# Two transformer layers on one core: three shifts of block 0 summed on TensorE, projections in the order q, q, k, k, v, v, and the first layer norms started elsewhere

## The chip, the core and the metric

The kernel runs on one core of one Trainium2 chip. The metric is the device time of one execution in microseconds; of several executions the median is given. The engines are TensorE (PE, with PEld for its weight loads), VectorE (DVE), ScalarE (ACT), GpSimd (POOL) and SyncE (SP), which here only issues DMAs. ScalarE and GpSimd issue DMAs too, in the same queue as their arithmetic.

## The reference

An activation `x` of 2048 positions x 1024 features (bf16) passes four residual steps: attention, gated MLP, attention, gated MLP, the two of a kind with the same weights. Each step normalizes its input first.

```python
def _A_ref(x, wqkv, wo):                 # H = 32 heads of 32
    W, dil = 8, 2
    qkv = (x @ wqkv) ...                 # q, k, v: heads x positions x 32
    off = jnp.arange(W) * dil
    idx = pos[:, None] - off[None, :]    # position s looks at s, s-2, ... s-14
    logits = einsum("bhsd,bhswd->bhsw", q, k[idx]) * scale
    logits = where(idx >= 0, logits, -1e9)
    o = einsum("bhsw,bhswd->bhsd", softmax(logits), v[idx])
    return o @ wo

def _B_ref(x, W_gate, W_up, W_down):     # 1024 -> 3584 -> 1024
    gate = x @ W_gate; up = x @ W_up
    return (gate * (gate > 0) * up) @ W_down

x = x + _A_ref(_layernorm(x)); x = x + _B_ref(_layernorm(x))
x = x + _A_ref(_layernorm(x)); x = x + _B_ref(_layernorm(x))
```

A head attends to eight positions only, two apart. Each of these eight distances is called a shift (`w` from 0 to 7).

## The kernel before

**Blocks.** The 2048 positions are four blocks of 512, each four tiles of 128 rows (`x_tiles`, kept in SBUF all along). The four residual steps are the layers L = 0 to 3, and a stage is written (L, b) for layer and block. TensorE goes through the first layer's projections of blocks 0, 1, 2, 3; wo of block 0 is put into the middle of block 3's projections; then the MLPs of the blocks follow, with the other wo products and the next layer's projections between them.

**Layer norm** (`plan_ln`, L208). ScalarE takes the sum and the sum of squares of each row tile (`stats`, two ACTIVATE passes, L221 and L222). For each pair of tiles VectorE turns them into mean and variance (`small_a`), GpSimd raises to the power -1/2 (L235), VectorE makes the bias (`small_b`), ScalarE normalizes (`norm`, L246), and SP issues a DMA transpose for two tiles (`turn`, L252). Its result, `xnT`, is what the matmuls read. Block 0's first layer norm has a class of its own (`First`): statistics on VectorE (BN stats), transposes on TensorE.

**Projections** (`plan_proj`, L356). Each of q, k and v has two slabs of 512 output features; a slab is four groups of 8 matmuls (128x128 weights, 512 positions), and each group is evicted from PSUM by ScalarE. q, k and v are feature-major there; ScalarE writes them to DRAM (`q_d`, `k_d`, `v_d`) and SP reads them back head-major (`qhm`, `khm`, `vhm`, L500), in four pieces each, with heads on partitions. GpSimd writes the last 14 positions of k and v for the next block.

**Attention** (`plan_attn`, L492). It is a chain on VectorE. For each shift: a multiply of q by the shifted k (L514, 128x4096), three adds (L524) and a fold (L531, L532) give the logits; then softmax (with the exponent on ScalarE), then for each of 8 groups of head features a multiply by the shifted v (L565) and adds; GpSimd writes the result to `o_d`, and SP reads it back as `oT`, which wo takes.

**Block 0 of layer 0** gets part of its logits another way (`first_logits`, L422): with q and k still feature-major, VectorE multiplies q by the k of several shifts at once (`mul`, L456), and TensorE adds up over the features of a head by matmuls with a matrix of ones and zeros (`wide`, 128x32, L468) into one PSUM tile. `NPE` is the number of shifts done so; the rest take the head-major path above.

**The order.** Nothing here is reordered at run time. A planner (`Plan`) gives each step a time from fixed costs (a matmul 0.216, a DVE step what its caller says, a landing 7.0) and sorts all steps by these times; the sorted list is what each engine's queue gets. `plan.on_pe` advances the clock of TensorE, `plan.on_dve` and `plan.chain` place VectorE's steps, `plan.slab` places weight loads in a ring of five buffers, and `plan.at` puts a step at a time. So a number in the code changes the place in a queue, not the time at which something runs. An engine waits in its queue for what its next instruction needs; SP too, whose DMAs also wait for earlier ones on the same completion counter.

**Buffers that the change touches.** `tpose` has four buffers for `xnT`, `oT` and the feature-major q and k; `ln_pool` has one buffer for the normalized rows of a block, so a layer norm waits for the transposes of the one before. `held` is the tile that later takes the MLP's hidden values and until then holds three of the six weight slabs of layer 0.

Of the kernel before, what the change touches and what calls it, by code (L numbers as in the profile page):

```python
# [9 lines left out]
BF16 = mybir.dt.bfloat16  # L10
# [22 lines left out]
NPE = 4  # L33
# [88 lines left out]
def kernel(  # L122
# [85 lines left out]
    def plan_ln(L, b, lag=0.5):  # L208
        hold = {}
        clock = [0.0]  # L210

        def stats(t):
            def f():
                if t == 0:
                    hold["xn"] = ln_pool.tile([P, TPB, D], BF16, tag="xn_all", name="xn_all")
                    hold["T"] = tpose.tile([P, TPB, KC, P], BF16, tag="T", name=f"xnT_{L}_{b}")
# [8 lines left out]
        def small_a(p):  # L225
            st = hold[("st", p)]
# [5 lines left out]
            vpe = stat_pool.tile([P, 2], F32, tag="vpe", name="vpe")  # L232
            nc.vector.tensor_scalar(vpe[:], nvar[:], -1.0 / D, EPS, op0=ALU.mult, op1=ALU.add)
            rstd = stat_pool.tile([P, 2], F32, tag="rstd", name="rstd")
            nc.gpsimd.tensor_tensor(rstd[:], vpe[:], neg_half[:, 0:2], op=ALU.pow)  # L235
            hold[("mean", p)], hold[("rstd", p)] = mean, rstd

        def small_b(p):
            nb = stat_pool.tile([P, 2], F32, tag="nb", name="nb")
            nc.vector.scalar_tensor_tensor(nb[:], hold[("mean", p)][:], -1.0, hold[("rstd", p)][:], op0=ALU.mult, op1=ALU.mult)  # L240
            hold[("nb", p)] = nb
# [16 lines left out]
        def row_done(t):  # L258
            def f(now):
                e = max(clock[0], now + 0.3)  # L260
                plan.at(e, stats(t))
                clock[0] = e + 2.6
# [7 lines left out]
        def after_b(now, t):  # L270
# [4 lines left out]
            plan.at(clock[0] + lag, turn(t))  # L275
# [80 lines left out]
    def plan_proj(L, b, hooks={}):  # L356
# [44 lines left out]
        for nm, g in (("q", 0), ("k", 0), ("q", 1), ("k", 1), ("v", 0), ("v", 1)):  # L401
# [20 lines left out]
    def first_logits(st, tm):  # L422
        hold = {}
        Ls = []
# [6 lines left out]
        def evict(nm, c, acc, t):  # L431
# [16 lines left out]
            if nm == "k":  # L448
                plan.chain.append((lambda: max(t + 0.7, reds.get(c - 4, 0.0) + 0.1), 1.2, mul(c), None))

        def mul(c):
            def f():
                if c % 2 == 0:
                    hold["pr"] = at_pool.tile([P, 2, NPE, BLK], BF16, tag="pr", name=f"prod_{c}", bufs=2)
                pr = hold["pr"][:, c % 2]
                nc.vector.tensor_tensor(pr, _ap(hold["q"], c * BLK, [[0, NPE], [1, BLK]]),  # L456
# [4 lines left out]
        def red(c0, n):  # L461
            def f():
                if c0 == 0:
                    Ls.append(psum.tile([P, NPE, P], F32, tag="acc", name="Lps"))
                for c in range(c0, c0 + n):
                    pr = hold.pop(("pr", c))
                    for tq in range(TPB):
# [12 lines left out]
        def step(c0, n):  # L480
            def f():
                e = plan.on_pe(1.0 + 1.13 * n, red(c0, n))
                for c in range(c0, c0 + n):
                    reds[c] = e
# [370 lines left out]
```

## Time and profile before

| what | value |
|---|---|
| median of 3 runs | 1630.16 us (1627.17 to 1630.46) |
| the profiled execution | 1631.8 us, of which the profile's span is 1630.1 |
| granted TensorE clock, mean | 0.998 |
| busy: PE, DVE, ACT, POOL | 1613.5, 1036.2, 459.2, 108.9 us |
| DMA | 319.14 MB, 196 GB/s on average |

In the page a line such as `L366 PE MATMUL acc_q<-xnT,wqk ... x32 [2.89 <-DMA xnT<-xn_all]` reads: line 366 of the kernel, engine, operation, output from inputs, number of instructions, and in brackets how long the engine sat idle before it and what ended that. A windows line gives, for a stretch of time, its length, the busy time of PE, PEld, DVE, ACT and POOL (with instruction counts), the granted clock of TensorE as a share of full speed, the DMA share and GB/s. SPq marks an instruction that issues a DMA, with the time that the issue took.

### The profile page before, as it was taken

The numbers are of one execution on the slowest core, as the hardware profiler recorded it, in microseconds if no ns is written. First come the engines' busy times: TensorE is split into PE (matmuls) and PEld (weight loads), VectorE is DVE, ScalarE is ACT, GpSimd is POOL, SyncE is SP. The second block draws the span as 40 slices with busy tenths as digits, with TensorE's granted clock in tenths as the row PEclk, the third lists the DMA queues.
The fourth block names the chain that finished last, engine by engine and source line by source line (L and its number), as shares of the span: only waits on it lengthen the run. The fifth ranks groups of instructions, "written<-read, shape, count | busy, mean of one in ns | idle before, by whom it ended". The sixth has DMA issues, their size and how long they took to land.

```text
span 1630.1 us, 19236 instructions
## 1 busy us (share of the span) xinstructions
PE 1613.5 (99%) x7609; PEld 740.4 (45%) x7658; DVE 1036.2 (64%) x1284; ACT 459.2 (28%) x734; POOL 108.9 (7%) x170
## 2 busy tenths in 40 slices
PE   9999999999999999999999999999999999999999
PEld 5443444444444444444444444444444444444444
DVE  3498989989999359880598716996989212211211
ACT  6564521404230341303413151133021301221110
POOL 2122000001000100011000110000000000000000
PEclk9999999999999999999999999999999999999999
DMA  8998668778955989569886699599846655565452
GB/s 258 224 195 179 188 175 206 207 195 208 240 165 192 256 191 237 153 217 232 198 215 176 206 238 209 160 278 241 219 149 198 197 168 162 174 178 158 155 166 67
DMA packets 456299, 319.14 MB, mean 196 GB/s; under 512 B 204016, under 2 KB 452240, under 8 KB 456208
## 3 DMA queue, kind: packets, MB, share of 16 engines
q1 hardware_dynamic: 424992, 283.60, 66.7%
q10 hardware_dynamic: 26544, 25.50, 5.4%
q0 software_dynamic: 4672, 8.80, 1.8%
q8 instruction: 60, 0.98, 0.3%
q14 instruction: 31, 0.25, 0.1%
HBM read 263.98 MB, written 38.15 MB: 185 GB/s over the span
## 4 chain that ended last, share of the span: by engine, by line
PE 95%; DMA 2%; DVE 1%; issue 0%; POOL 0%; SPq 0%; ACT 0%; DVEq 0%; POOLq 0%
PE acc_u L676 24%; PE acc_g L676 24%; PE dacc L722 24%; PE acc_wo L646 7%; PE acc_k L366 6%; PE acc_q L366 6%; PE acc_v L366 6%; DMA xnT<-xn_all 1%; DVE l L524 0%; DMA khm<-k_d 0%; DMA v_d<-stage_v 0%; DVE pr L514 0%; DMA x<-in_A_x_dram 0%; POOL rstd L235 0%; DVE bst L296 0%
## 5 line engine op out<-in xcount | busy, mean ns | idle before, releaser
L676 PE MATMUL acc_u<-xnT,wu 128*128 128x512 bf16 x1792 | 423.3, 379 | 0.0
L676 PE MATMUL acc_g<-xnT,wg 128*128 128x512 bf16 x1792 | 423.3, 379 | 0.0
L722 PE MATMUL dacc<-wd,hT 128*128 128x512 bf16 (+1 forms) x1787 | 386.4, 376 | 1.7
L691 DVE TENSOR_TENSOR hT<-acc_u,r 128x512 bf16<-128x512 f32 x224 | 154.3, 689 | 323.8 <-PE acc_u L676 317.8
L683 ACT ACTIVATE r<-acc_g 128x512 bf16<-128x512 f32 x224 | 133.6, 597 | 708.0 <-PE acc_g L676 702.3
L722 PEld LDWEIGHTS <-hT 128*128 128x128 bf16 x1820 | 178.1, 98 | 209.0
L676 PEld LDWEIGHTS <-wg 128*128 128x128 bf16 x1792 | 175.4, 98 | 211.4
L676 PEld LDWEIGHTS <-wu 128*128 128x128 bf16 x1792 | 175.3, 98 | 211.4
L514 DVE TENSOR_TENSOR pr<-qhm,khm 128x4096 bf16<-128x4096 bf16 x60 | 137.0, 2284 | 35.7 <-DMA x<-in_A_x_dram 21.5
L524 DVE TENSOR_TENSOR l<-l,pr 128x1024 f32<-128x1024 f32 x120 | 146.6, 1222 | 2.6
L565 DVE TENSOR_TENSOR pvt<-a,vhm 128x4096 bf16<-128x4096 bf16 x64 | 146.2, 2284 | 0.2
L730 DVE TENSOR_TENSOR x<-dacc,x 128x512 bf16<-128x512 f32 (+1 forms) x65 | 42.7, 679 | 122.2 <-PE dacc L722 122.0
L366 PE MATMUL acc_k<-xnT,wk 128*128 128x512 bf16 x512 | 113.3, 379 | 0.0
L646 PE MATMUL acc_wo<-wo,oT 128*128 128x512 bf16 x496 | 111.0, 379 | 0.8
L366 PE MATMUL acc_v<-xnT,wv 128*128 128x512 bf16 x384 | 84.2, 379 | 0.0
L221 ACT ACTIVATE xn_all<-x 128x1024 bf16<-128x1024 bf16 x60 | 63.2, 1054 | 66.5 <-DVE x L653 62.7
L573 DVE TENSOR_TENSOR pvt<-pvt 128x2048 bf16<-128x2048 bf16 x64 | 78.1, 1221 | 1.2
L246 ACT ACTIVATE xn_all<-x,nb,rstd 128x1024 bf16<-128x1024 bf16 x60 | 71.9, 1233 | 21.1 <-DVE nb L240 16.6
L646 PEld LDWEIGHTS <-oT 128*128 128x128 bf16 x512 | 50.1, 98 | 60.4
L366 PEld LDWEIGHTS <-wk 128*128 128x128 bf16 x512 | 50.0, 98 | 60.4 <-issue 0.4
L375 ACT CAST stage_q<-acc_q 128x512 bf16<-128x512 f32 x56 | 32.4, 581 | 159.1 <-PE acc_q L366 155.3
L576 POOL DMA_DIRECT2D o_d<-ohm x64 | 35.4, 553 | 617.0 <-DVE ohm L575 602.1
(76 smaller groups left out, 884.9 us busy)
## 6 DMA issues: line engine op xcount, KB each, us to landing
wg<-in_B_W_gate_dram SPq DMA_DIRECT2D x56, 1024.0 KB, 7.5
wu<-in_B_W_up_dram SPq DMA_DIRECT2D x56, 1024.0 KB, 5.5
wd<-in_B_W_down_dram SPq DMA_DIRECT2D x48, 1024.0 KB, 6.3
wo<-in_A_wo_dram SPq DMA_DIRECT2D x16, 1024.0 KB, 7.1
wk<-in_A_wqkv_dram SPq DMA_DIRECT2D x10, 1024.0 KB, 5.4
wv<-in_A_wqkv_dram SPq DMA_DIRECT2D x9, 1024.0 KB, 5.9
khm<-k_d SPq DMA_DIRECT2D x32, 284.0 KB, 8.5
vhm<-v_d SPq DMA_DIRECT2D x32, 284.0 KB, 7.0
```

The source lines that it names most:

```text
L221: nc.scalar.activation(junk, xt[:], ACT.Identity, accum_out=st[:, 0, t % 2:t % 2 + 1])
L246: nc.scalar.activation(hold["xn"][:, t, :], x_tiles[b * TPB + t][:], ACT.Identity, scale=rstd[:, i:i + 1], bias=nb[:, i:i + 1])
L366: nc.tensor.matmul(acc[:, t0 * P:t1 * P], lhsT=w["t"][:, kc, j * P:(j + 1) * P], rhs=xnT[(L, b)][:, t0:t1, kc, :], start=(kc == 0), stop=( ...
L514: nc.vector.tensor_tensor(pr[:], st["q"][:], _ap(st["k"], HALO - DIL * w, [[HALO + P, DH], [1, P]]), op=ALU.mult)
L524: nc.vector.tensor_tensor(l[:], pr[:, 0:8] if i == 0 else l[:], pr[:, 8 * i + 8:8 * i + 16], op=ALU.add)
L565: nc.vector.tensor_tensor(tt[:], a_bc, v_sh, op=ALU.mult)
L573: nc.vector.tensor_tensor(tt[:, 0:4], tt[:, 0:4], tt[:, 4:8], op=ALU.add)
L646: nc.tensor.matmul(acc[:], lhsT=st["oT"][:, c, t, :], rhs=ws[half]["t"][:, c, :], start=(c == 0), stop=(c == KC - 1))
L676: nc.tensor.matmul(acc[:], lhsT=w["t"][:, kc, (j % 4) * P:(j % 4 + 1) * P], rhs=xnT[(L, b)][:, :, kc, :], start=(kc == 0), stop=(kc == KC ...
L683: nc.scalar.activation(r[:], hold.pop(("g", j))[:], ACT.Relu)
L691: nc.vector.tensor_tensor(st["hT"][:, j, :], hold.pop(("u", j))[:], hold.pop(("r", j))[:], op=ALU.mult)
L722: nc.tensor.matmul(accs[(t, c0)][:], lhsT=st["hT"][:, j, t * P:(t + 1) * P], rhs=w["t"][:, jl, c0 - half * SLAB:c0 - half * SLAB + n], sta ...
```

## The change

`NPE` goes from 4 to 3: in block 0 of layer 0, three shifts are summed on TensorE and shift 3 takes the head-major path. The sums, before in two batches (after the first group of k's second slab, and after v's first slab), are one batch after v's first slab; so all eight products must be kept until then, in `held`, in the tile `l1`, in the buffer of `vhm` and in two `pr` tiles. In all layers the projections run q, q, k, k, v, v, before q, k, q, k, v, v. The x rows of blocks 2 and 3 are loaded early. The first layer norm of block 1 takes its statistics on VectorE by BN stats; those of block 2 and block 3 are planned about a block earlier. Block 0's q and k pieces are planned sooner and closer together. wo of block 0 stands behind the third group of k's first slab in block 3, which is group 11 of the new order, before group 8.

```diff
-NPE = 4
+NPE = 3
...
-    def plan_ln(L, b, lag=0.5):
+    def plan_ln(L, b, on_vector=False):
...
+        def bn(t):
...
+                for h in range(2):
+                    nc.vector.bn_stats(hold[("bn", t // 2)][:, t % 2, h, :], x_tiles[b * TPB + t][:, 512 * h:512 * h + 512])
...
         def small_a(p):
...
+            if on_vector:
+                mv = stat_pool.tile([P, 2, 2], F32, tag="mv2", name="mv2")
+                for i in range(2):
+                    nc.vector.bn_aggr(mv[:, i, :], hold[("bn", p)][:, i].rearrange("p a b -> p (a b)"))
+                nc.vector.tensor_scalar(vpe[:], mv[:, :, 1], EPS, None, op0=ALU.add)
+                nc.gpsimd.tensor_tensor(rstd[:], vpe[:], neg_half[:, 0:2], op=ALU.pow)
...
-                plan.at(e, stats(t))
-                clock[0] = e + 2.6
+                if on_vector:
+                    plan.on_dve(e, 1.4, bn(t))
+                    clock[0] = e + 1.4
+                else:
+                    plan.at(e, stats(t))
+                    clock[0] = e + 2.6
...
-            plan.at(clock[0] + lag, turn(t))
+            plan.at(clock[0] + 0.5, turn(t))
...
-        for nm, g in (("q", 0), ("k", 0), ("q", 1), ("k", 1), ("v", 0), ("v", 1)):
+        for nm, g in (("q", 0), ("q", 1), ("k", 0), ("k", 1), ("v", 0), ("v", 1)):
...
-                plan.chain.append((lambda: max(t + 0.7, reds.get(c - 4, 0.0) + 0.1), 1.2, mul(c), None))
+                plan.chain.append((lambda: t + 0.7, 1.2, mul(c), None))
...
+                if c == 0:
+                    pr = held[:, 3 * KC:3 * KC + NPE, :]
+                elif c == 1:
+                    pr = at_pool.tile([P, NPE, BLK], BF16, tag="l1", name="prod_1")
+                else:
+                    if c == 2:
+                        hold["pr"] = hm_pool.tile([P, 2, NPE, BLK], BF16, tag="v", name="prod_2")
+                    elif c % 2 == 0:
+                        hold["pr"] = at_pool.tile([P, 2, NPE, BLK], BF16, tag="pr", name=f"prod_{c}", bufs=2)
+                    pr = hold["pr"][:, c % 2]
...
-        def step(c0, n):
-            def f():
-                e = plan.on_pe(1.0 + 1.13 * n, red(c0, n))
...
-        return {"evict": evict, ("k", 1, 0): step(0, 4), ("v", 0, 3): step(4, 4)}
+        def step():
+            plan.at(plan.on_pe(8.0, red) + T_EV, out)
+
+        return {"evict": evict, ("v", 0, 3): step}
...
-                load(ends["q"] + 6.0, (("q", q_d, BLK, P),), 2.0)
-                tm["qk_in"] = load(ends["k"] + 6.0, (("k", k_d, ROW, HALO + P),), 2.0)
+                load(ends["q"] + 5.5, (("q", q_d, BLK, P),), 1.5)
+                tm["qk_in"] = load(ends["k"] + 4.0, (("k", k_d, ROW, HALO + P),), 1.5)
...
-            hooks = {("k", 0, 3): lambda: wo(0, 0)} if L == 0 and b == NB - 1 else {}
+            hooks = {("k", 0, 2): lambda: wo(0, 0)} if L == 0 and b == NB - 1 else {}
...
-    plan.at(9.0, consts_late)
+    plan.at(14.0, consts_late)
...
-            plan.at(-4.5 if b == 1 else 41.5 * (b - 1) + 1.0 * (t % TPB), load_x(t))
+            plan.at((-4.5, -1.5, 20.5)[b - 1], load_x(t))
...
-        if b + 1 < NB:
-            late_ln(0, b + 1, plan.pe + 9.0, 0.5 if b == 0 else 8.0)
+        if b == 0:
+            late_ln(0, 1, plan.pe + 7.0, on_vector=True)
+            late_ln(0, 2, plan.pe + 30.0)
+        elif b == 1:
+            late_ln(0, 3, plan.pe + 15.0)
         proj(0, b)
```

## The prediction

> **What bounds the kernel now.** I read the page's busy table first, then the waits by engine, then the timeline and the windows around the waits that TensorE has, last the queues that feed them.
>
> ```profile
> PE 1613.5 (99%) x7609; PEld 740.4 (45%) x7658; DVE 1036.2 (64%) x1284; ACT 459.2 (28%) x734; POOL 108.9 (7%) x170
> PE acc_q L366 <- DMA xnT<-xn_all: 6.9, 2, 4.0
> 99.43 8.75 PE L366 MATMUL acc_q<-xnT,wqk 128*128 128x512 bf16 x32 [2.89 <-DMA xnT<-xn_all]
> 146.71 8.75 PE L366 MATMUL acc_q<-xnT,wqk 128*128 128x512 bf16 x32 [4.00 <-DMA xnT<-xn_all]
> ```
>
> TensorE is busy for 1613.5 of 1630.1 us, so the change can matter in two ways only: through the 16.6 us in which TensorE idles, or through the speed of its matmuls. The second line (what TensorE waited for) says where 6.9 us of the idle time lie: twice, on the transposed rows `xnT`, at the first projection of block 2 (99.4 us) and of block 3 (146.7 us). Each wait is followed by 32 matmuls that take 8.75 us, where the same 32 take 6.91 elsewhere in the chain that ended last. The windows say why:
>
> ```profile
> 99.00:100.00 1.00, 0.57 (x3) 0.32 (x4) 0.93 (x3) 0.00 (x0) 0.03 (x1) 0.97 1.36 151
> 100.00:101.00 1.00, 1.00 (x4) 0.30 (x2) 0.97 (x2) 0.00 (x0) 0.00 (x0) 0.50 1.29 276
> 102.00:103.00 1.00, 1.00 (x4) 0.36 (x3) 0.48 (x1) 1.00 (x3) 0.00 (x0) 0.50 0.83 135
> 104.00:105.00 1.00, 1.00 (x6) 0.41 (x5) 0.95 (x1) 0.78 (x2) 0.47 (x1) 1.00 0.85 250
> ```
>
> The seventh number is the granted clock: 0.50 for some 3.5 us after the wait. So a wait costs its length and 8.75 - 6.91 = 1.84 us more.
>
> The rest of the chain into these waits is late by its order. Block 2's layer norm starts with ScalarE's sums at 64.26 us, after x rows that SP issues only at 57 to 68 us, and its second transpose is issued at about 91 us and lands at 99.4. ScalarE and VectorE are not short of time there: VectorE idles 21.5 us up to 66.3, waiting for block 0's k pieces.
>
> ```profile
> 66.29 2.29 DVE L514 TENSOR_TENSOR pr<-qhm,khm 128x4096 bf16<-128x4096 bf16 x1 [21.45 <-DMA x<-in_A_x_dram]
> 60.90 0.54 SPq L500 DMA_DIRECT2D khm<-k_d  x1
> 132.63 8.79 SPq L252 DMA_TRANSPOSE xnT<-xn_all  x2
> 184.56 7.70 SPq L252 DMA_TRANSPOSE xnT<-xn_all  x2
> 203.65 1.89 PE L676 MATMUL acc_g<-xnT,wg 128*128 128x512 bf16 x8
> ```
>
> The last two lines are the place to watch: the transposes of block 0's second layer norm, which must land before the gate matmuls.
>
> **The change, part by part.** *TensorE's own work.* The same projections run in another order; at 6.91/4 = 1.727 us for a group of 8 matmuls this costs nothing. The shift sums were 2 x 16 matmuls of 512 columns; each batch delays the next group by 0.97 us (33.88 to 34.85, 47.05 to 48.02), 1.94 together. Now 32 of 384 columns run at once: 1.94 x 384/512 = 1.46 if time follows columns, 1.94 if it doesn't. I take 1.46, saving 0.5 (bounds 0 and 0.5).
>
> *Layer norm of block 1.* Eight ACTIVATE passes (1.06 us and 0.19 for the read) leave ScalarE: 10 us less. VectorE gets 8 BN stats of 0.64 (two take 1.29) and 4 aggregates of 0.21, 6 us. They stand ahead of the products in VectorE's queue, where VectorE waited 6.82 us for the first k eviction, which now comes 6.9 us later still (second q group first). ScalarE then normalizes between q evictions until about 31 us, and the transposes land, at 7 us each, before 40; block 1 needs them at 54.3. Cover 14 us.
>
> *x early.* Eight 256 KB loads pass from 57-68 and 98-103 us to before 35 us; four stand ahead of block 1's transposes on SP. At the 350 GB/s that the DMA moves early, four take 3 us, out of that cover.
>
> *Layer norms of blocks 2 and 3.* Block 2's sums now start once the last k is evicted. TensorE's times: second slab at 18.24 (as now), k from 25.15, v from 38.97, sums to 47.4, block 1 at 54.3, block 2 at 54.3 + 24 x 1.727 = 95.8, block 3 at 137.2. On ScalarE from 39.8: four rows of 2.5, four v evictions of 0.58, DMA issues and a copy, to 53.5; up to 2.5 more if a v write has to await a k piece's landing, since that write follows in the same queue. Then VectorE's small steps (0.7), the POOL power, four norms of 1.24: transposes issued by 64, landed by about 71, or by 75 at the slowest landing of the whole trace (10.8). Needed: 95.8. Block 3's follow a block later, 40 us ahead of need. Both waits go: 2.89 + 1.84 + 4.00 + 1.84 = 10.57 us.
>
> One term of this has a rule against it. The row first: after 2.89 us of idling the clock was 0.50. The Trainium skill ("TensorE: Matmul & The Clock Gate", Part 1: The HAM clock gate, "What's actually happening") puts the drop at an idle window of about 3.4 us or more. By that rule the first wait, at 2.89, would cost no slow matmuls and the gain would be 1.84 less; the row shows it does, so I keep 10.57.
>
> *One shift more on VectorE.* Products: 8 x (1.18 - 0.89) = 2.4 us less, under idle time. But shift 3 goes through the head-major path: a multiply 2.29, three adds 3.7, folds 1.44, so 7.5 us more in a VectorE chain that is over 90% busy from here to 480 us. Its start moves too. Block 0's q pieces are issued right after the transposes (before 42), the k pieces once the last k write (40.1, landing 5.7) is in: 46 to 48, landed by 53 to 57. But block 2's small steps stand ahead in VectorE's queue, waiting for the sums: start T = 55 to 59.5, taken as 58 (now 66.3). Now this chain takes 66.3 to 144.9 = 78.6 us; with shift 3 (+7.5) and two small steps fewer (-1.9) it is 84.2: end at 142.2, 2.7 earlier than now.
>
> *wo of block 0, three groups later.* TensorE comes to it at 137.2 + 11 x 1.727 = 156.2 (now 162.2). o_d lands some 4 us after the end and an oT piece 3 to 5 later: the first at about 151. Cover 5 us; pieces 2 to 4 are needed 3.45 us apart. The gate weights wait on SP for the second q slab's release at 151.0, ahead of the last oT piece: that piece lands at 156, needed at 166.5.
>
> *What is late next.* The eight wo groups end at 170.0, and 13 projection groups later, at 192.5, the gate matmuls need `xnT_1_0`: 22.5 us after wo, now 27.5. VectorE from 142.2: two shifts 15.0, then to the last x add 16.0 (multiplies 2 x 2.3, eight adds of 0.69, fold, three l adds, small step): 173.2, where TensorE alone would allow 171. ScalarE's sums to 176.3, then norms and k evictions in turn to 183.7; the last transpose is issued then. The two now landed 5.3 to 7.0 after issue: 189 to 191. Slack 1.5 to 3.5, or minus 2 at the 10.8 landing; SP issues one 1 MB weight load just ahead of it. I take the stall at nothing. If this cover goes, TensorE waits up to 3 us, and 1.84 more if the wait nears 2.9. The wo of block 1 had oT pieces landed 10 us ahead; TensorE comes 11 us earlier, VectorE at least 2.7 (it waits 6.6 us for TensorE between 200 and 320, and can give that back): about 5 left. Later stages have more.
>
> The POOL power took 0.70 us beside an idle VectorE and 1.54 to 2.60 beside the multiplies; block 2's moves from beside them to before them, the rest stay, so it adds nothing.
>
> **Sum.** 10.57 + 0.5 = 11.1 us off the profiled execution: 1631.8 (span 1630.1 and 1.7 around it) becomes 1620.7. The median of the runs, 1630.16, is 1.64 below that execution, so the forecast is 1630.16 - 11.1 = 1619.1 us.
>
> **The rivals.** *A new wait at the gate matmuls or at wo of block 0* (0.24): the slack above is thin and rests on T. For: VectorE paces the last x adds in the new order. Against: the same transposes now land 7 us early. Price 1 to 3 us, or up to 5 with the slow clock: 1620 to 1624.
>
> *One wait stays* (0.05), the change not doing what it says: a transpose is issued early, but SP holds it behind queued work, as SP now holds the second one of block 3 (8.79 us for two). One wait of 5.84 back: 1625.
>
> *Slower* (0.07): VectorE's chain becomes the bound. Beyond T of about 60 every us delays the last x adds and so the gate matmuls, plus 1.84 for the clock. To lose the 11.1 and 3.3 more, T must reach 60 + 14.4 - 1.8 = 72.6, which is 6 later than the start now, with k pieces blocked behind loads and writes. Against: the x loads that sat between the k pieces are gone. Time 1633 to 1640.
>
> **How the numbers follow.** The forecast has 0.64. The unit for "same" is 0.2%, 3.3 us, which is also the spread of the three runs. Faster holds the forecast, the first rival and half of the second (1625 is only 1.8 past that unit): 0.90. Same gets the other half and the mildest of the slower rival, 0.04; slower the rest, 0.06. The range: the low end is 1619.1 less 2.6, since one of the runs shown lies that much below the others; the high end, 1625, takes in the gate wait with its slow clock and one wait that stays.
>
> **What would show it.** Right: no TensorE wait on `xnT` at blocks 2 and 3, 6.91 us in place of 8.75, granted clock 1.00 there; block 2's first matmul near 95.8 us and block 3's near 137.2; one batch of sums of about 1.5 us; VectorE's first L514 multiply at 55 to 60 us; wo of block 0 near 156.2 and the gate matmuls near 192.5, with no wait. Wrong: a wait of TensorE at L676 or L646, a first L514 after 62 us, or a clock of 0.50 anywhere after the start.

## The result, and the profile after

| | before | after |
|---|---|---|
| median | 1629.01 us (10 runs, 1623.57 to 1633.42) | 1635.99 us (10 runs, 1634.51 to 1638.29) |
| ratio after / before | | 1.0049, 95% interval 1.0033 to 1.0064 |
| the profiled execution (span) | 1631.8 (1630.1) | 1636.91 (1635.2) |

The change makes the kernel slower by 0.5%, where 1619.1 us was forecast. The page's busy table comes first, then what TensorE waited for (us in total, number of waits, the longest):

```profile
PE 1617.6 (99%) x7658; PEld 741.1 (45%) x7658; DVE 1045.1 (64%) x1297; ACT 448.6 (27%) x718; POOL 102.5 (6%) x170
```

```profile
PE acc_g L695 <- DMA xnT<-xn_all: 6.6, 1, 6.6
PE acc_wo L665 <- DMA oT<-o_d: 2.8, 2, 1.5
...
PE acc_v L391 <- ACT stage_k L400: 1.1, 2, 0.8
PE acc_q L391 <- ACT stage_v L400: 1.0, 2, 0.7
```

The two waits for `xnT` at L366, 6.9 us together, are gone as forecast. New ones have come, 11.5 us together: for oT at wo, for transposed rows at the first gate matmuls (those of the first MLP, called the gate below), and for PSUM that ScalarE evicts late. TensorE's timeline (start, length, instruction, idle time before it) shows the last part:

```profile
159.84 3.63 PE L665 MATMUL acc_wo<-wo,oT 128*128 128x512 bf16 x16
164.92 7.08 PE L665 MATMUL acc_wo<-wo,oT 128*128 128x512 bf16 x32 [1.46 <-DMA oT<-o_d]
173.31 3.63 PE L665 MATMUL acc_wo<-wo,oT 128*128 128x512 bf16 x16 [1.31 <-DMA oT<-o_d]
...
205.97 3.57 PE L695 MATMUL acc_g<-xnT,wg 128*128 128x512 bf16 x8 [6.59 <-DMA xnT<-xn_all]
212.28 1.89 PE L695 MATMUL acc_g<-xnT,wg 128*128 128x512 bf16 x8
```

and the windows there have the granted clock as seventh number:

```profile
202.00:203.00 1.00, 0.00 (x0) 0.00 (x0) 0.97 (x2) 0.00 (x0) 0.00 (x0) 0.50 1.28 237
206.00:208.00 2.00, 2.00 (x5) 0.66 (x6) 0.89 (x1) 0.00 (x0) 0.00 (x0) 0.50 1.09 349
212.00:214.00 2.00, 2.00 (x11) 0.88 (x9) 1.45 (x2) 0.00 (x0) 0.00 (x0) 1.00 0.00 0
```

The wait at the gate costs 6.59 us and, through the clock, 2.86 more: from the first to the second group of gate matmuls it takes 6.31 us, in the kernel before 3.45. A sum over one stretch closes the account. From block 1's first projection (54.94 before, 54.22 after) to the second gate group (207.10 and 212.28) both kernels do the same matmuls. It takes 152.16 us before, of which 10.57 are the two waits and their slow clock; so 141.6 are work. After, it takes 158.06: 16.5 us are lost. The waits listed above make 11.5, the slow clock 2.9, and shorter pieces some 2. The balance, 16.5 - 10.57 - 0.72 (the sooner start) = 5.2 us, is the difference of the two profiled executions, 5.1. The medians differ by 7.0: the profiled execution of the kernel before lies 2.8 us above its median, that of the changed kernel 0.9, and these 1.9 us lie outside the two traces. Behind the gate the two take the same time: from the second gate group to the end it is 1423.0 us before and 1422.9 after.

Why is everything late? VectorE's head-major chain starts at 68.77, not at 58 (this start is called T below). The chain of waits that ends in it, from 15 to 70 us (start, length, what):

```profile
23.70 11.26 DMA x<-in_A_x_dram
34.95 9.09 DMA xnT<-xn_all
...
44.12 0.37 ACTq L467
...
60.54 2.27 DMA v_d<-stage_v
62.81 0.02 issue
62.83 0.54 SPq L519
63.37 0.04 issue
63.41 5.19 DMA khm<-k_d
...
68.77 2.31 DVE pr L533
```

Two steps in it connect transfers that share no data. ScalarE's write of k at 44.12 follows the landing of block 1's second transpose; and the third k piece, read back by SP at 62.83, follows the landing of a **v** write. Both are waits for a completion counter. The DMAs of SP and ScalarE take eight counters in turn, and a DMA waits until the earlier one with the same counter has landed. The order with the counter of each DMA, from the trace of the changed kernel (T1: transposes of block 1; k, v, q1: ScalarE's writes; x, qhm, khm: SP's loads):

```
T1.7  q.0  T1.1  k.2  x.3  x.4  k.5  x.6  x.7  qhm.0  k.1  k.2  qhm.3  v.4  qhm.5
v.6  qhm.7  v.0  khm.1  v.2  q1.3  q1.4  q1.5  khm.6  q1.7  khm.0  khm.1
```

The third k write takes counter 1 behind T1.1, the third k piece counter 0 behind the third v write; the fourth stands behind it on SP. In the kernel before, its own chain has the same three steps with the fourth v write:

```profile
55.76 5.12 DMA v_d<-stage_v
60.88 0.02 issue
60.90 5.22 DMA khm<-k_d
...
66.29 2.30 DVE pr L514
```

So in both kernels the transfer that ended last before the final k piece was a v write, not an x load and not one of k's own writes. In the changed kernel an x load and a transpose stand further back in the chain: they hold ScalarE, whose v writes then come late.

### The profile page after: what moved, and what is told of

Its sections match the earlier page's. It is cut to its first block, busy times and chain, and to the rows that moved or that the text cites. A ratio compares the mean times of both kernels' runs of the same rounds, so it can differ in the third digit from the quotient of the medians.

```text
span 1635.2 us, 19283 instructions
## 1 busy us (share of the span) xinstructions
PE 1617.6 (99%) x7658; PEld 741.1 (45%) x7658; DVE 1045.1 (64%) x1297; ACT 448.6 (27%) x718; POOL 102.5 (6%) x170
## 4 chain that ended last, share of the span: by engine, by line
PE 92%; DMA 3%; DVE 2%; SPq 1%; ACT 1%; issue 0%; ACTq 0%; DVEq 0%
PE acc_g L695 24%; PE acc_u L695 24%; PE dacc L741 24%; PE acc_wo L665 6%; PE acc_k L391 5%; PE acc_q L391 5%; PE acc_v L391 5%; DMA xnT<-xn_all 1%; DVE l L543 1%; SPq L791 1%; DMA x<-in_A_x_dram 1%; DVE pr L533 1%; DMA oT<-o_d 1%; DMA k_d<-stage_k 0%; SPq L198 0%
## 5 line engine op out<-in xcount | busy, mean ns | idle before, releaser
L391 PE MATMUL acc_q<-xnT,wq 128*128 128x512 bf16 x384 | 84.2, 379 | 0.0
L391 PE MATMUL acc_k<-xnT,wk 128*128 128x512 bf16 x384 | 84.2, 379 | 0.0
L234 ACT ACTIVATE xn_all<-x 128x1024 bf16<-128x1024 bf16 x56 | 59.0, 1053 | 81.4 <-DVE x L672 72.6
L543 DVE TENSOR_TENSOR l<-pr 128x1024 f32<-128x1024 bf16 x61 | 74.3, 1218 | 0.8
```

Source lines behind the costliest of these rows:

```text
L234: nc.scalar.activation(junk, xt[:], ACT.Identity, accum_out=st[:, 0, t % 2:t % 2 + 1])
L391: nc.tensor.matmul(acc[:, t0 * P:t1 * P], lhsT=w["t"][:, kc, j * P:(j + 1) * P], rhs=xnT[(L, b)][:, t0:t1, kc, :], start=(kc == 0), stop=( ...
L543: nc.vector.tensor_tensor(l[:], pr[:, 0:8] if i == 0 else l[:], pr[:, 8 * i + 8:8 * i + 16], op=ALU.add)
```

## The experiments

In all of them the 30 transposes of layer-normed rows are plain copies of the same 512 KB from the same tile to the same tile, in pieces of 512 bytes (the first expectation says 128 to 512; it was 512 throughout). Rows then stand where columns should, so values differ; the order of the DMAs of SP and of ScalarE is that of the original kernels, and so are their counters, but for one pair that swaps them in the changed kernel (three pairs in `c_after_slow_copies`).

```diff
-                nc.sync.dma_start_transpose(hold["T"][:, t - 1:t + 1].rearrange("p t k n -> p (t k) n"),
-                                            hold["xn"][:, t - 1:t + 1].rearrange("p t d -> p (t d)"))
+                nc.sync.dma_start(_ap(hold["T"], (t - 1) * D, [[256, 8], [1, 256]]),
+                                  _ap(hold["xn"], (t - 1) * D + 1792, [[-256, 8], [1, 256]]))
```

Runs of one group (A to F) were on one chip. The kernel before ran in each group, at medians of 1632.7, 1631.7, 1627.8, 1629.5, 1632.2 and 1630.0, so groups are compared by the ratio to it. T, the end of the last x add of block 0's wo, the first gate matmul and the wait before it are from the profile of one execution. The changed kernel with copies was run twice, with T at 68.95 and at 66.58, so some 2 us in T are no more than what two executions of one kernel differ by.

| run | group | median | ratio (95%) | T | last add | gate | wait |
|---|---|---|---|---|---|---|---|
| c_before | A | 1626.05 | 0.9964 (0.9949-0.9978) | 67.27 | 171.99 | 198.69 | 0 |
| c_after | A | 1627.78 | 0.9980 (0.9964-0.9996) | 68.95 | 182.71 | 201.27 | 2.27 |
| c_after_x2_behind | A | 1628.83 | 0.9989 (0.9972-1.0006) | 67.55 | 181.31 | 199.88 | 1.87 |
| c_after_two_shifts_off | A | 1631.70 | 1.0007 (0.9994-1.0021) | 67.36 | 181.42 | 201.17 | 6.54 |
| c_after_k_together | B | 1629.12 | 0.9989 (0.9980-0.9997) | 61.61 | 178.63 | 199.03 | 5.66 |
| c_after_x2_behind_k_together | B | 1628.43 | 0.9975 (0.9963-0.9987) | 61.37 | 178.48 | 198.93 | 5.80 |
| c_before_k_together | B | 1631.64 | 1.0003 (0.9992-1.0015) | 65.49 | 176.18 | 202.91 | 0 |
| c_before_wo_later | C | 1622.60 | 0.9956 (0.9941-0.9972) | 67.36 | 177.04 | 197.82 | 0 |
| c_after_up_slab_behind | C | 1624.27 | 0.9970 (0.9954-0.9986) | 64.34 | 178.11 | 197.59 | 0 |
| c_after_k_together_wo_back | C | 1621.09 | 0.9951 (0.9930-0.9971) | 60.65 | 172.88 | 194.13 | 0 |
| c_k_together_wo_back_four | C | 1622.88 | 0.9965 (0.9949-0.9981) | 59.12 | 177.03 | 194.93 | 0 |
| c_after_second | D | 1626.45 | 0.9985 (0.9971-0.9999) | 66.58 | 180.35 | 198.66 | 0.38 |
| c_after_k_by_gpsimd | D | 1620.55 | 0.9942 (0.9923-0.9961) | 61.05 | 174.81 | 193.08 | 0.42 |
| c_after_x2_behind_k_by_gpsimd | D | 1620.57 | 0.9940 (0.9920-0.9961) | 60.94 | 174.71 | 193.82 | 0 |
| c_before_second | E | 1626.01 | 0.9965 (0.9951-0.9979) | 66.96 | 171.69 | 197.46 | 0 |
| c_before_k_by_gpsimd | E | 1628.45 | 0.9981 (0.9971-0.9991) | 65.57 | 172.98 | 199.71 | 0 |
| c_after_slow_copies | F | 1631.64 | 1.0017 (1.0002-1.0032) | 64.35 | 178.10 | 200.89 | 5.97 |
| c_after_k_by_gpsimd_slow_copies | F | 1627.22 | 0.9990 (0.9976-1.0005) | 61.01 | 174.77 | 197.84 | 5.34 |

### The first theories: SP's queue, and the third shift

Before any run, the queue theory: block 2's x loads ahead of block 1's transposes on SP make T late. Its rival: the third shift makes the chain too long.

> The kernel before, with each of its 30 transposes of the layer-normed rows replaced by a plain copy of the same 512 KB from the same tile to the same tile, in pieces of 128 bytes to 512 bytes; rows then stand where columns should, so the values differ. It is the baseline of the runs with copies. A copy needs less of SP than a transpose (an x load of half the bytes takes 1.3 us of SP, a transpose 1.9 to 2.9), so the waits of TensorE on xnT at blocks 2 and 3 (2.89 and 4.00 us in the kernel before) may shrink: 1620 to 1632 us. The first head-major multiply stays near where it is in the kernel before.

> The changed kernel with the same copies for its transposes; its DMAs share their completion counters as in the changed kernel. Queue theory: the copy of block 1's second pair of tiles still stands behind block 2's four x loads, ScalarE's third k write waits for it, and the first head-major multiply comes at 64 to 69 us instead of 58; slower than the kernel before with copies by 0 to 8 us. Shift theory (the third shift's 7.5 us on VectorE is what makes the chain late, wherever it starts): the multiply can come at 58 to 62 us and the time is still 4 to 8 us over the kernel before with copies. Transpose theory (the 13.3 us landing behind a 1 MB load is what costs): no wait of more than 1 us at the first gate matmul, and 5 to 8 us less than the changed kernel's 1636.

```diff
-            plan.at((-4.5, -1.5, 20.5)[b - 1], load_x(t))
+            plan.at((-4.5, 20.4, 20.5)[b - 1], load_x(t))      # c_after_x2_behind
```

> The changed kernel with copies, and block 2's four x loads issued behind block 1's two copies instead of ahead of them; nothing else is changed. Queue theory: ScalarE no longer stands still at its third k write, the first head-major multiply comes 5 to 10 us sooner than with the loads ahead (58 to 61 us), the first wo matmul no longer waits for oT, and the time falls by 4 to 10 us. Shift theory: the multiply may come sooner, but the time changes by less than 2 us. A cost on the other side: block 2's layer norm now starts later by the loads' 5 us, which a wait of TensorE on xnT at block 2 would show.

```diff
-NPE = 3
+NPE = 4      # c_after_two_shifts_off: four shifts on TensorE again
```

> The changed kernel with copies, and TensorE summing four shifts of block 0 as before the change, still in one go (the products of four shifts take more of VectorE before the head-major part, and its head-major part is one multiply and its tree shorter, 7.5 us). Shift theory: the first wo and the first gate no longer wait, and the time falls by 6 to 11 us against the changed kernel with copies. Queue theory: the head-major part still starts as late, its end moves 5 to 7.5 us sooner, so oT's wait (2.8 us) goes and the gate's wait shrinks by no more than 3 us, while the sums take 0.4 us more of TensorE; the time falls by 2 to 5 us.

With copies the change costs 1.7 us instead of 7.0, and T is as late as in the changed kernel. Both theories fell. With the loads behind, ScalarE's k writes were all issued by 40.75, not 45.02, yet T came only 1.4 us sooner, within what two executions differ by, and the time did not fall (+1.05 us). With four shifts the wait for oT went, but the gate waited longer, on VectorE's last add that was as late as ever, and the time rose by 3.9 us:

```profile
67.36 2.29 DVE L533 TENSOR_TENSOR pr<-qhm,khm 128x4096 bf16<-128x4096 bf16 x1 [9.53 <-DMA khm<-k_d]
```

```profile
201.17 3.60 PE L695 MATMUL acc_g<-xnT,wg 128*128 128x512 bf16 x8 [6.54 <-DMA xnT<-xn_all]
```

The reason is in the order of VectorE's instructions: with one shift less in block 0, the planner put one more shift of block 1 ahead of the x adds.

### The counter

The k pieces 0.1 us apart in the plan follow each other in the list, with counters 2, 3, 4, 5, and only the first v write stands in front (the expectations below call the third v write the last one).

```diff
-                tm["qk_in"] = load(ends["k"] + 4.0, (("k", k_d, ROW, HALO + P),), 1.5)
+                tm["qk_in"] = load(ends["k"] + 4.0, (("k", k_d, ROW, HALO + P),), 0.1)
```

> The changed kernel with copies in pieces of 512 bytes for its transposes; the four head-major k pieces of block 0 are planned 0.1 us apart instead of 1.5, so that they follow each other among the DMAs and the last of them takes over its completion counter from the first v write of the block instead of the last. Counter theory (the last k piece waits for the counter of block 0's last v write, 59.93 plus 2.8 us in the run with copies, and that alone holds the first head-major multiply at 68.95): the pieces wait for the last k write (45.0 plus some 5 us) and the first v write (48.8 plus some 5), so the multiply comes at 59 to 62 us, SP comes to block 2's copies before 62 instead of at 70, the waits for oT at the first wo go, and the time falls by 3 to 8 us against the changed kernel with copies (1627.8, ratio 0.998: to a ratio of 0.993 to 0.996). Queue theory as first put (ScalarE's stall behind block 1's copies sets it): the multiply stays at 66 or later and the time changes by less than 2 us. Shift theory: the multiply comes sooner, the time falls by less than 2 us.

> As the run with the k pieces together, and block 2's four x loads behind block 1's copies. In the run with the loads behind alone ScalarE's four k writes were done 4.3 us sooner (last issue 40.75 instead of 45.02), and yet the first head-major multiply came only 1.4 us sooner, at 67.55. Counter theory: with both, the multiply comes at 54 to 59 us, since neither the k writes nor the v writes are late any more; no wait for oT, ScalarE's evictions of block 1 no longer late by more than 1 us; 4 to 9 us less than the changed kernel with copies. Queue theory as first put: no more than 2 us less than the run with the k pieces together. Shift theory: less than 2 us off the changed kernel with copies, with a wait for oT or at the gate still in place.

> The kernel before with copies in pieces of 512 bytes, and its four head-major k pieces of block 0 planned 0.1 us apart instead of 2.0. In the run of before with copies the last k piece was issued at 62.14, after the last v write (issue 56.15), and the multiply came at 67.27. Counter theory: the pieces now wait for the second and third v writes (issue 48.2 and 52.7) and the multiply comes at 61 to 64; the time stays within 2 us of the 1626 of before with copies, since TensorE there waits only for xnT at block 3 (3.38 us) and not for VectorE. If the multiply stays at 67, the counter of the v write isn't what held it.

T came to 61.61 as the counter theory said, and the waits for oT went (wo at 156.96), but the time didn't fall: the gate now waited 5.66 us. Moving the x loads as well added nothing clear (0.9975 against 0.9989). VectorE's list tells why again. The k pieces planned sooner changed its order: from T to the last x add it has 128 instructions in place of 121 (two adds of block 1 and five small steps of a layer norm more), and a block 1 multiply stands between the third and the fourth x add. So T came 7.3 us sooner but the last add only 4.1. In the kernel before, T moved by 1.8 us only, less than the 3 to 6 expected: the third v write (52.67, landing in 4.54) and a landing of 7.55 us of the last piece held it; the time rose (0.9964 to 1.0003) with a wait of 5.54 us for `xnT` at block 3, so the 2 us expected of it were wrong too.

### wo three groups later, and the slab between the copies

```diff
-            hooks = {("k", 0, 3): lambda: wo(0, 0)} if L == 0 and b == NB - 1 else {}
+            hooks = {("q", 1, 2): lambda: wo(0, 0)} if L == 0 and b == NB - 1 else {}   # c_before_wo_later
```

> The kernel before with copies in pieces of 512 bytes, and one part of the change alone: the output projection of block 0 follows the eleventh projection group of block 3 instead of the eighth, which leaves 13 groups (22.5 us) instead of 16 (27.6) between it and the first gate matmul, and lets the second up slab (1 MB) come between the two copies of the layer norm on SP. Cover theory: from the end of wo to the landing of the layer norm's second copy it takes 24 to 29 us in every run so far, so the gate now waits 2 to 7 us for xnT, the clock falls behind that wait, and the time rises by 3 to 9 us over before with copies (ratio 0.9964 then: to 0.998 to 1.002). If the layer norm has room, as the forecast had it (slack 1.5 to 3.5 us), the time changes by less than 2 us.

```diff
-                      "u": slab(wu_v[:, :, c0:c0 + SLAB], f"wu_{L}_{b}_{j // 4}")}
+                      "u": slab(wu_v[:, :, c0:c0 + SLAB], f"wu_{L}_{b}_{j // 4}",
+                                172.2 if (L, b, j) == (1, 0, 4) else -10.0)}         # c_after_up_slab_behind
```

> The changed kernel with copies in pieces of 512 bytes, and the second up slab of block 0 (1 MB) issued behind both copies of the layer norm that feeds the first gate, instead of between them. In the run with copies the second copy was issued at 192.64, 3 us behind the slab, and landed at 201.3, 8.6 us later; TensorE waited 2.27 us and then ran eight matmuls in 3.57 us instead of 1.89. Transpose theory (the load just ahead is what makes the copy late): it lands 4 to 6 us after its issue, the wait at the gate goes, and the time falls by 2 to 5 us against the changed kernel with copies (ratio 0.998). Cover theory: the copy is issued no sooner, and lands at 197 or later: the wait shrinks, but 0 to 2 us of it can stay. If the landing stays over 8 us, the slab isn't what slows it.

```diff
-            hooks = {("k", 0, 2): lambda: wo(0, 0)} if L == 0 and b == NB - 1 else {}
+            hooks = {("q", 1, 3): lambda: wo(0, 0)} if L == 0 and b == NB - 1 else {}   # with 0.1 above; ..._four also NPE = 4
```

> As the run with the k pieces together, and wo of block 0 back behind the eighth group of block 3, as before the change (16 groups, 27.6 us to the gate; both copies of the layer norm then stand ahead of the second up slab). With the pieces together alone oT was in time (wo at 156.96), but the gate waited 5.66 us and the time stayed at 1629. Cover theory: wo comes to 152 to 155, waits for oT by 0 to 3 us, the wait at the gate falls below 1.5 us, the slow clock behind it goes, and the time falls by 4 to 8 us against that run (ratio 0.9989: to 0.994 to 0.9965). Shift theory: VectorE's chain, 7.5 us longer, makes TensorE wait 4 us or more for oT at wo, and the time falls by less than 3 us.

> As the run with the k pieces together and wo back, and TensorE sums four shifts as before the change, in one go: 0.5 us more of TensorE, 7.5 us less of VectorE's head-major part. Of the change there stay the order q, q, k, k, v, v, the early x loads, the sooner layer norms with one on VectorE, and the sums in one go. Cover theory with the chain early: no wait of more than 1 us between block 1 and the gate; the first gate matmuls at 193 to 196 us; the time 5 to 9 us under the run with the k pieces together alone, and under before with copies. Shift theory: it is faster than the same with three shifts by 3 to 7 us; without it, by -1 to 2 us.

The cover theory (13 projection groups between wo and the gate are too few for the layer norm that the gate needs) fell in its plain form: in the kernel before, wo three groups later costs nothing (0.9956 against 0.9964), the gate comes 22.3 us after wo without a wait. There VectorE keeps pace with wo, and its last add ends 1.5 us after it:

```profile
161.56 13.98 PE L646 MATMUL acc_wo<-wo,oT 128*128 128x512 bf16 x62
197.82 1.89 PE L676 MATMUL acc_g<-xnT,wg 128*128 128x512 bf16 x8
```

In the changed kernel the adds end 5.6 us after wo (182.53 against 176.94), since VectorE is in block 1's multiplies. With T early and wo back the gate's wait goes and 0.8 us of waits for oT are left; the ratio is 0.4% under that of the pieces together alone. With four shifts it is not faster than with three. The slab behind the copies made them land in 3.7 us (median) and the gate did not wait; its T was 64.34, though the edit touches nothing ahead of T, and the ratio, 0.997 against 0.998, is not told apart.

### T alone

The changed kernel and the eight runs that keep three shifts, the 1.5 us and wo behind the eleventh group have VectorE's instructions in one and the same order around the adds, and in all nine the last add ends at T + 113.75 to 113.77 (68.77 to 182.53, 67.55 to 181.31, 64.34 to 178.11, 61.05 to 174.81). The next edit moves T and leaves that order and the plan as they are: in the traces GpSimd's DMAs have eight counters of their own. (Four DMAs fewer on SP also shift the turn of the counters behind them, so T is not strictly the only thing that moves.)

```diff
-                    nc.sync.dma_start(st[nm][32 * tq:32 * tq + 32, :, :],
+                    eng = nc.gpsimd if (nm, L, b) == ("k", 0, 0) else nc.sync
+                    eng.dma_start(st[nm][32 * tq:32 * tq + 32, :, :],
```

> The changed kernel with copies in pieces of 512 bytes once more, as the baseline of the two runs beside it (the kernel before itself moves by some us from chip to chip, so runs are compared within one group). Chain theory: from the first head-major multiply (T) to the last x add VectorE has 113.8 us of work in a fixed order (68.95 to 182.7 in the first run of this kernel, 67.55 to 181.3 with the x loads behind, 64.34 to 178.1 with the up slab behind), so the last add ends at T + 113.8 again, whatever T is, and the gate comes 18 to 19 us after it, or at 197 where that is later.

> The changed kernel with copies, and the four head-major k pieces of block 0 issued by GpSimd instead of SP; GpSimd's DMAs have completion counters of their own, so no piece waits for the counter of a v write. The order of SP's other DMAs around the first gate and the order of VectorE's instructions are the same as in the changed kernel with copies; wo stays behind the eleventh group, and three shifts are summed. The last piece stands on GpSimd behind the halo of the second v write (ScalarE, 54.7). Chain theory: T at 58 to 63, the last x add at T + 113.8 = 172 to 177, no wait for oT at wo, the wait at the gate under 2 us, and the time 3 to 8 us under the changed kernel with copies of the same group. Cover theory (13 groups are too few behind wo, whatever T): the gate still waits 4 to 6 us, the time changes by less than 2 us. Shift theory: VectorE's longer chain still makes wo or the gate wait 2 us or more.

> As the run with the k pieces by GpSimd, and block 2's four x loads behind block 1's copies, so that ScalarE's k and v writes are not held either (the second v write was at 50.5 in the run with the loads behind, against 54.7). This gives the T of the forecast. Chain theory: T at 55 to 59, the last x add at 171 to 173 (TensorE's end of wo bounds it there), wo near 156, the gate near 192.5 to 194 with no wait over 1 us, and the time 6 to 11 us under the changed kernel with copies of the same group: then T is the one term of the forecast that failed. Cover theory: a wait of 4 us or more at the gate. Shift theory: a wait of 2 us or more for oT.

GpSimd issues the pieces at 50 to 55 us, and VectorE starts 5.5 us sooner than in the run beside it, `c_after_second` (GpSimd's timeline, then VectorE's and TensorE's; the lines of this kernel stand one further down):

```profile
50.27 1.59 POOL L520 DMA_DIRECT2D khm<-k_d  x2 [4.05 <-DMA qhm<-q_d]
52.56 0.81 POOL L520 DMA_DIRECT2D khm<-k_d  x1
...
54.10 0.80 POOL L520 DMA_DIRECT2D khm<-k_d  x1
```

```profile
61.05 2.29 DVE L534 TENSOR_TENSOR pr<-qhm,khm 128x4096 bf16<-128x4096 bf16 x1 [5.17 <-DMA v_d<-stage_v]
...
173.53 1.28 DVE L673 TENSOR_TENSOR x<-acc_wo,x 128x512 bf16<-128x512 f32 x2
```

```profile
156.24 13.98 PE L666 MATMUL acc_wo<-wo,oT 128*128 128x512 bf16 x62
193.08 1.89 PE L696 MATMUL acc_g<-xnT,wg 128*128 128x512 bf16 x8 [0.42 <-DMA xnT<-xn_all]
```

These are the forecast's numbers: wo 156.2, last add 173.2 (174.81 here), gate 192.5. The time falls by 5.9 us to 1620.55. It is won ahead of the gate. The run beside it, with T at 66.58, waited at wo and had its slow clock there, and came to the gate 5.6 us later; the wait at the gate itself is as short:

```profile
PE acc_wo L665 <- DMA oT<-o_d: 2.4, 2, 1.9
170.51 5.31 PE L665 MATMUL acc_wo<-wo,oT 128*128 128x512 bf16 x15 [1.95 <-DMA oT<-o_d]
198.66 1.89 PE L695 MATMUL acc_g<-xnT,wg 128*128 128x512 bf16 x8 [0.38 <-DMA xnT<-xn_all]
```

Three shifts and wo three groups later stay as they were: with T early, and VectorE in this order, neither costs anything that shows. With the x loads behind as well nothing more is gained.

> The kernel before with copies in pieces of 512 bytes once more, as the baseline of the run beside it. It waits for xnT at the first projection of block 3 (3.38 us in the first run) with a slow clock behind it in some executions: ratio 0.9945 to 0.998 to the kernel before.

> The kernel before with copies, and its four head-major k pieces of block 0 issued by GpSimd: the same edit that brought the changed kernel with copies from 1626.45 to 1620.55. Chain theory: VectorE's first head-major multiply comes to 57 to 62 instead of 67.3, but TensorE waits here for block 2's and 3's layer norms, whose x loads and transposes stay late on SP, so the time falls by no more than 3 us; the changed kernel with the k pieces by GpSimd (ratio 0.9942) stays 2 to 6 us faster than this one, and that is what the change itself is worth once its chain starts in time. If this one falls to 1621 as well (ratio 0.9945 or less), the edit did it alone and the change is worth nothing even then.

The same edit on the kernel before makes it slower by 2.4 us, so it is no gain by itself. T was expected at 57 to 62 and came at 65.57: the pieces were issued by 55.7, but landed in 8.0 us (median; 6.3 in the changed kernel), beside block 2's x loads at 53 to 59, which the change has moved away. With both, the changed kernel is faster by 0.4% (0.9942 against 0.9981). Against the kernel before with copies and without this edit (0.9964 and 0.9965) it is 0.2%, and the intervals overlap.

### The landing of the last copy

```diff
+                m = 64 if (L, b) == (1, 0) else 256       # pieces of 128 bytes at the layer norm before the first gate
```

> The changed kernel with copies, and only the two copies of the layer norm that feeds the first gate in pieces of 128 bytes instead of 512, to make them land later, as the transposes do: in the changed kernel the last transpose landed 13.3 us after its issue, the copy 8.4 us after. Chain theory with the landing as a second term: the last x add again at T + 113.8, the last copy issued 10 us after it, and for each us that it lands later than 8.4 us after its issue the gate waits one us more, with 1.7 to 2.9 us of slow clock once the wait passes some 2 us. At a landing of 12 to 14 us the gate waits 4 to 7 us and the time is 5 to 9 us over the changed kernel with copies (ratio 0.9985 then: to 1.001 to 1.004). If the landing doesn't matter, the ratio stays within 0.0015.

> The same slow copies at that one layer norm, with the k pieces by GpSimd, so that the chain starts near 61 us and the last copy is issued at 184.7 while TensorE comes to the gate at 192.7. If T alone were the failed term, the gate would still not wait for more than 1 us and the ratio stay at 0.994. If the landing is a second one: at 12 to 14 us the copy lands at 197 to 199, the gate waits 4 to 6 us, and of the 5.9 us that the earlier chain gave the kernel with quick copies 0 to 2 are left against the kernel before with copies (1626, ratio 0.9965): a ratio of 0.9965 to 0.999, still 4 to 8 us under the changed kernel with slow copies.

With the slow copies the last one takes 12.55 us to land instead of 8.20 (chains of the run with the chain in time and of its quick twin):

```profile
185.15 12.55 DMA xnT<-xn_all
```

```profile
184.75 8.20 DMA xnT<-xn_all
```

```profile
197.84 3.55 PE L697 MATMUL acc_g<-xnT,wg 128*128 128x512 bf16 x8 [5.34 <-DMA xnT<-xn_all]
```

Even with T at 61.01 the gate then waits 5.34 us and the ratio goes from 0.9942 to 0.9990. So T is not the only term that failed. With the late chain the gate waited 5.97 us, and the ratio went from 0.9985 to 1.0017:

```profile
188.41 1.26 SPq L274 DMA_DIRECT2D xnT<-xn_all  x1
200.89 3.57 PE L696 MATMUL acc_g<-xnT,wg 128*128 128x512 bf16 x8 [5.97 <-DMA v_d<-stage_v]
```

The timeline names a v write there, but it was the slow copy: it landed 12.34 us after its issue, at 200.75, just before the matmul; TensorE waits for its counter there, and no v write landed between 198.2 and 202.4. Between these two runs, on one chip, the chain in time is worth 4.4 us (T was 64.35 and 61.01). With the slow copies the changed kernel is 0.5% above the kernel before with copies (1.0017 against 0.9964), as much as the change cost with transposes.

## Why the prediction was wrong, step by step

- **The two waits at blocks 2 and 3, 10.57 us:** right. Both are gone, and the granted clock there is 1.00. At block 2 about 1 us of waits for PSUM took their place. And the price was read in one execution. The kernel before took 1623.5 to 1636.0 us over all groups, the mean granted clock falling from 1.000 to 0.995 along with it, which suggests that its waits differ from one execution to the next.
- **One batch of sums:** right; it took 1.5 us, and block 1 started at 54.22 (54.3 forecast).
- **x early, "out of that cover":** mis-priced. It was weighed against TensorE's need at 54.3 alone. The transposes landed at 44.1 instead of 40, and behind them stood ScalarE's third k write, for a counter; ScalarE idled for 7.04 us. What this cost T is not told apart from nothing: 1.4 us in the runs with copies, where two executions of one kernel differ by 2.4.
- **"One shift more on VectorE", start T = 55 to 59.5, taken as 58:** the first step that failed. Its reason was that the k pieces go out once the last k write is in, and that only the x loads between them had held them. T was 68.77. The last pieces wait for a v write, which no data require. The prediction blamed the x loads between the pieces, and an x load is the name that the timeline gives to VectorE's idle time in the kernel before; the chain of waits that ends in the same multiply names the v write. The late chain brought the waits for oT at wo (2.8 us) and those for PSUM (2.1 us, in no term of the sum): with T at 61.05, in the runs with copies, TensorE has neither. The length of the chain from T was right: 84.2 forecast, 84.0 measured, and to the last add 115.2 against 113.76.
- **wo at 156.2 with a cover of 5 us, gate at 192.5:** right from T on. The run with T at 61.05 has 156.24 and 193.08.
- **The landing of the last transposes, 5.3 to 7.0 us, with the slab "just ahead of it", the stall at nothing:** the second step that failed, at 6.59 us of wait and 2.86 of slow clock. SP's timeline and the chain in the changed kernel:

```profile
188.69 1.89 SPq L273 DMA_TRANSPOSE xnT<-xn_all  x1
190.68 1.04 SPq L198 DMA_DIRECT2D wu<-in_B_W_up_dram  x1
192.50 7.16 SPq L273 DMA_TRANSPOSE xnT<-xn_all  x1
```

```profile
192.50 13.34 DMA xnT<-xn_all
```

The 1 MB load was between the two transposes, and the second took 7.16 us on SP and 13.34 to land. TensorE came at 199.38; with a landing of 7.0 it would have waited 0.1. So the 6.59 us are the landing's for the most part, and an early chain would not have saved them: with T at 61.01 a landing of 12.55 still cost 5.34 us, and with T at 66.58 one of 8.23 cost 0.38. The late chain costs ahead of the gate, where TensorE came 6.9 us later than the 192.5 of the forecast. In the runs with copies each was worth about as much as the other: the chain 4.4 us (slow copies) to 5.9 (quick ones), each within one group; the landing, across groups and so by the ratio, 0.3% (0.9985 to 1.0017) to 0.5% (0.9942 to 0.9990), some 5 to 8 us.

That the load just ahead is what made the real transpose slow is shown for copies alone. The bound of 7.0 came from the two transposes at that place in the kernel before. The same trace has transposes that landed in 9.3 to 10.1 us with no 1 MB load just ahead on SP; the one at block 2 was issued at 89.2, not at about 91 as the prediction reads (the pair there; the last number is the slowest landing):

```profile
DMA to landing us min/median/max: 6.4/8.3/10.1
```

- **The rivals.** The gate wait had its mechanism right and its price too low (1 to 5 us). The slower rival named the late chain as the one thing that turns the sign, with k pieces blocked behind loads and writes, but asked for T of 72.6, because it left the slow landing out; with it, 68.8 was enough.

What stays open: no run has the k pieces by GpSimd, or the slab behind, together with real transposes, so why that one transpose landed so late is not shown, and how the loss splits there is argued from the copies. No run has the earlier layer norms alone in the kernel before. The slow copies suggest that an early chain alone would bring the changed kernel about level with the kernel before (0.9990), still 0.3% above the kernel before with copies.

## What to carry to other kernels

When an engine idles, follow the chain of waits that ends in its next instruction, and not only the name beside the idle time; hold each name against the time at which that transfer landed, and look at each step for a transfer that shares no data with the next, because a shared completion counter moves with every reordering of DMAs. A step that is moved ahead has to be priced against everyone who waits behind it, also behind its counter. And where the sum has a start time that every later term rests on, its upper bound is the number to prove first.

## What the runs showed of the hardware

- **Completion counters join independent queues.** In the kernel before SP stood idle from 57.89 to 60.90 us ahead of a k read, until a v write landed; in the changed kernel ScalarE idled for 7.04 us ahead of a k write, until a transpose that SP had issued landed. The Trainium skill (DMA: Bandwidth & Descriptors, "Why a DMA increments its semaphore by 16 and not by 1") asks for one semaphore for each slot in flight, since two transfers on one can't be told apart; the rows show what that costs when eight slots go round.
- **The clock fell after waits of about 2 us.** A wait of 2.27 us was followed by eight matmuls in 3.57 us in place of 1.89, at a granted clock of 0.57 to 0.58 (c_after); one of 1.95 by fifteen in 5.31 in place of 3.63, with the clock at 0.50 from 172 to 174 us (c_after_second, at wo); one of 1.87 by eight in 1.89, at 1.00 (c_after_x2_behind). The Trainium skill (TensorE: Matmul & The Clock Gate, Part 1) puts the drop at about 3.4 us of idle time; by that none of them would have had it.
- **A load just ahead of a copy doubled its landing.** The copies ahead of the gate landed in 3.6 and 3.8 us with the 1 MB load behind both (c_after_up_slab_behind); with the load between them the first landed in 4.0 and the second, just behind it, in 8.2 (c_after_second).
